# Another order of the set-up, and new planning keys for the first and last steps, in a kernel of memory attention and gated layers on one core

## The chip, the core and the metric

The kernel runs on one core of one Trainium2 chip. A core has TensorE for matrix products, VectorE, ScalarE and GpSimd for elementwise work, and SyncE, which here only issues DMAs; 16 DMA engines move data between the chip's main memory and the on-chip buffers. Matrix products are written to PSUM, eight banks of 128 x 512 f32, and must be copied from there by VectorE or ScalarE. The metric is the device time of one execution in microseconds (us), and smaller is better. In the views PE is TensorE's matmul row, PEld its weight loads, DVE is VectorE, ACT is ScalarE, POOL is GpSimd, SP is SyncE; SPq and ACTq are the DMA issues of SyncE and ScalarE.

## The reference

Four layers are applied to x (2048 x 448) in turn, each with a layer normalization in front and a sum with its input behind: A, B, A, B, the same weights both times.

```python
def _A_ref(x, mem0, Wq, Wk, Wv, Wo, seg_len):      # H = 16 heads, Dh = 256, M = 8, seg_len = 32
    mem = mem0
    for s in range(n_seg):                          # 64 segments, one after the other
        h = concatenate([mem, x[:, 32*s : 32*s+32]], axis=1)
        q, k, v = (einsum('btd,dhe->bhte', h, W) for W in (Wq, Wk, Wv))
        scores = where(mask, einsum('bhqe,bhke->bhqk', q, k) * Dh**-0.5, -1e9)
        o = einsum('bhqk,bhke->bhqe', softmax(scores), v)
        o = einsum('bhte,hed->btd', o, Wo)
        mem = o[:, :M]                              # the next segment's memory
        outs.append(o[:, M:])
def _B_ref(x, W_gate, W_up, W_down):                # F = 1792
    return (relu(x @ W_gate) * (x @ W_up)) @ W_down
```

The memory makes A a recurrence: segment s + 1 can't be scored before segment s has given its eight memory rows.

## The kernel before

**Set-up (`setup`, L672).** Since q and k, and v and Wo, meet only in products, the kernel first multiplies the weights out: M = Wq Wk^T for each head (448 x 448, kept in `Mw` and, for the last 64 of 448 rows, `M3`) and N = Wv Wo for each head (`Nw`). Each of the four weights comes in four quarters of four heads. A quarter of Wq, Wk or Wv is loaded by one transposing DMA (`load_t`, L691, issue L692), a quarter of Wo by a plain one (`load_o`, L695, issue L696). All are issued by SyncE: first Wq and Wk alternately, then Wv and Wo alternately. They land in space that is used for something else later: in `Nw` (Wq, half of Wk, one quarter of Wo) and in `big` (the rest), which later holds the gate layers' weights and the buffer U. TensorE works through M's four quarters (`full` and `pair3`, called from L764 on), then N's (`n_main`, `n_last`, L788 and L796). A unit is one 128 x 448 result in a PSUM bank and one copy by ScalarE (L867) or VectorE (L868). All these matmul groups write a common key, `("stage",)`, so they keep the order of the program among themselves.

**Steps.** Step t works on segment t of the first A layer and, from t = 4 (`LAG`), on segment t - 4 of the second: 68 steps, of which the first four and the last four have one A layer only. A step is: `t_block` (M and M3 times the segment's 40 rows, results TTm and TTs), `s_mem` (scores and softmax of the memory rows, Em and Pm), `p_t_mem` (its transpose PTm), `u_mem` (probabilities times rows, UTm), `un_mem` (112 matmuls of UTm with all of N, L1162), the new memory `mv` (L1180), and `m_t`, which hands it to the next step. Beside that chain the segment's own rows go through `s_seg`, a transposing DMA `PTs` and `u_seg` into U. Every second step does `un` (U times N, 64 rows), a normalization (`ln_b`, whose transposition by DMA is `xBT`) and a gate layer (`b_layer`, `b_down`). In steps 0 and 1 and in the last, `fill` (L969) puts in matmuls of `Mw` with `ident` whose result nobody reads.

**Who sets the order.** All operations are added to `_Order` (L307) in program order, with resources read and written, and `run` places them by a greedy plan with fixed costs per operation: on each engine the operation with the earliest due time goes first among those that can start soon. The due time is `o.key`. A matmul group of a step takes it from the table `SLOT` (L174); the table has keys of their own for steps 0 to 3 (suffix a0 to a3) and for the last four (z0 to z3, z5), and for all others one set of four (0 to 3) that repeats every four steps. Anything without an entry, the DMAs of the set-up among them, is due as early as the earliest of its followers wants, less a latency and its own cost (L374):

```python
o.key = min([q.key - (0.0 if o.kind == q.kind == "pe" else lat + 60.0) for q in o.succs], default=1e9) - min(o.cost.values())
```

From step 8 to 63 the matmul groups are tied to one line in the order of their keys. A change of the matmuls' tile shape (`mode`) is planned at 95 ns.

**Gate weights.** They come in 21 pieces (`S.pieces`, issue L816). A piece is released by a matmul group: in step 0 by those named in `PACE[0]` (L873: p_t_mem, u_mem, un_mem, m_t), in step 1 by most groups. Each also waits until N's groups have read the space (`free`, L785).

Of the kernel before, what the change touches and what calls it, by code (L numbers as in the profile page):

```python
# [6 lines left out]
BF = dt.bfloat16  # L7
# [5 lines left out]
D = 448  # L13
# [16 lines left out]
LAG = 4  # L30
NP = (NSEG + LAG) // 2
# [14 lines left out]
class _Sched:  # L46
# [260 lines left out]
class _Order:  # L307
# [13 lines left out]
    def add(self, kind, eng, cost, fn, rd, wr, name=None, mode=0, lat=None, alt=None, base=(0, 0)):  # L321
# [5 lines left out]
        if kind == "pe" and o.cat:  # L327
            name = o.cat + o.sub
            i = self.count[name] = self.count.get(name, -1) + 1
            o.slot = f"{name}.{i}@" + (f"a{o.t}" if o.t < LAG else f"z{o.t - NSEG}" if o.t >= NSEG else str(o.t % 4))  # L330
# [1118 lines left out]
```

## Time and profile before

| | |
|---|---|
| time, three runs | 1523.01 us median (1522.46 to 1526.68) |
| profiled execution | span 1524.4 us; the page gives no other time of it |
| PE / PEld busy | 1473.0 us (97%) / 1155.9 us (76%) |
| DVE / ACT / POOL busy | 790.8 / 783.1 / 112.3 us |
| mean granted clock of TensorE | 0.993 |
| memory read and written | 10.33 and 1.84 MB |
| first M unit, first unit of N, first t_block of step 1 | at 11.0, 45.0 and 78.98 us |
| steps 8 to 15 | 172.7 us, 21.6 a step |

The profile is of one execution. A row of a timeline reads: start, length, engine, line, operation, out<-in by the program's names, shape, count, and in brackets the idle time before it and what ended it. Most rows bear the line of a helper (L139 for all matmuls, L867 and L868 for copies), so they are told apart by their tiles: `b<-hT,Mw` is a t_block, `b<-Nw,UTm` is un_mem, `b<-big` of 128x448 in the first 72 us is a product of the set-up. A row of a window reads: stretch, length, busy time and count of PE, PEld, DVE, ACT and POOL, TensorE's granted clock, share of the DMA engines, GB/s. An SPq row is the time that SyncE spent issuing a DMA, not the time until it landed. "issue" as releaser means that the profile shows nothing that was waited for.

### The profile page before, as it was taken

The numbers are of one execution on the slowest core, as the hardware profiler recorded it, in microseconds if no ns is written. First come the engines' busy times: TensorE is split into PE (matmuls) and PEld (weight loads), VectorE is DVE, ScalarE is ACT, GpSimd is POOL, SyncE is SP. The second block draws the span as 40 slices with busy tenths as digits, with TensorE's granted clock in tenths as the row PEclk, the third lists the DMA queues.
The fourth block names the chain that finished last, engine by engine and source line by source line (L and its number), as shares of the span: only waits on it lengthen the run. The fifth ranks groups of instructions, "written<-read, shape, count | busy, mean of one in ns | idle before, by whom it ended". The sixth has DMA issues, their size and how long they took to land.

```text
span 1524.4 us, 82710 instructions
## 1 busy us (share of the span) xinstructions
PE 1473.0 (97%) x38178; PEld 1155.9 (76%) x38178; DVE 790.8 (52%) x2131; ACT 783.1 (51%) x2510; POOL 112.3 (7%) x259
## 2 busy tenths in 40 slices
PE   6989899999999999999999999999999999999998
PEld 2567777888787787878787787878777787878786
DVE  5435445645554555545554554545455564555554
ACT  5734554555545555554555455554555555455443
POOL 4000000000000000000000000000000000000000
PEclk9999999999999999999999999999999999999999
DMA  9851011100000101111010110011010110001010
GB/s 212 198 128 25 16 16 21 22 16 18 21 20 15 27 17 21 18 18 22 16 23 17 22 22 16 18 22 22 17 23 17 21 22 14 20 16 20 17 24 15
DMA packets 137738, 47.86 MB, mean 31 GB/s; under 512 B 125736, under 2 KB 137264, under 8 KB 137392
## 3 DMA queue, kind: packets, MB, share of 16 engines
q1 hardware_dynamic: 137040, 42.33, 13.8%
q8 instruction: 300, 4.92, 1.4%
q14 instruction: 46, 0.38, 0.1%
q10 hardware_dynamic: 352, 0.24, 0.1%
HBM read 10.33 MB, written 1.84 MB: 8 GB/s over the span
## 4 chain that ended last, share of the span: by engine, by line
PE 79%; DVE 8%; DMA 7%; SPq 3%; ACT 2%; issue 1%
PE b L139 79%; DMA PTs<-Ps 3%; SPq L692 2%; DMA xBT<-xn 2%; ACT Em L1073 1%; DVE UTm L868 1%; DMA ride<-mv 1%; SPq L1215 1%; ACT Es L1116 1%; DVE stat L1117 1%; DVE big L868 1%; DVE Es L1115 1%; DVE Ps L1119 1%; DMA big<-in_A_Wk_dram 1%; DVE stat L1114 1%
## 5 line engine op out<-in xcount | busy, mean ns | idle before, releaser
L139 PE MATMUL b<-hT,Mw 128*128 128x80 bf16 (+1 forms) x11424 | 438.0, 200 | 0.2 <-issue 0.2
L139 PEld LDWEIGHTS b<-hT,Mw 128*128 128x128 bf16 x11424 | 420.1, 100 | 17.5 <-issue 1.8
L139 PE MATMUL b<-Nw,big 128*32 128x448 bf16 (+1 forms) x3924 | 300.0, 354 | 0.6 <-DMA Nw<-in_A_Wo_dram 0.6
L867 ACT ACTIVATE TTs<-b 128x320 bf16<-128x320 f32 (+5 forms) x670 | 283.3, 423 | 5.3 <-PE b L139 5.0
L867 ACT ACTIVATE TTm<-b 128x80 bf16<-128x80 f32 (+5 forms) x671 | 156.5, 233 | 238.7 <-PE b L139 232.7
L139 PE MATMUL b<-xBT,big 128*128 128x128 bf16 (+3 forms) x4900 | 212.6, 215 | 2.8 <-DMA xBT<-xn 2.0
L139 PEld LDWEIGHTS b<-Nw,big 128*32 128x32 bf16 (+1 forms) x3924 | 129.7, 97 | 99.5 <-issue 10.9
L139 PE MATMUL b<-Nw,UTm 128*32 128x224 bf16 x7504 | 196.8, 263 | 4.2 <-ACT UTm L867 1.6
L139 PEld LDWEIGHTS b<-xBT,big 128*128 128x128 bf16 (+1 forms) x4900 | 184.5, 101 | 19.9 <-issue 3.9
L139 PEld LDWEIGHTS b<-Nw,UTm 128*32 128x32 bf16 x7504 | 178.3, 98 | 25.8 <-DVE UTm L868 13.4
L867 ACT ACTIVATE big<-b 128x512 bf16<-128x512 f32 (+1 forms) x218 | 111.4, 564 | 81.3 <-PE b L139 81.0
L868 DVE CAST TTm<-b 64x64 bf16<-64x64 f32 (+4 forms) x213 | 46.5, 219 | 198.2 <-PE b L139 195.4
L139 PE MATMUL b<-hT,M 64*128 64x80 bf16 (+3 forms) x3808 | 142.1, 197 | 2.9 <-issue 1.2
L868 DVE CAST big<-b 128x512 bf16<-128x512 f32 (+1 forms) x170 | 96.3, 589 | 74.3 <-PE b L139 74.2
L139 PEld LDWEIGHTS b<-hT,M 64*128 64x128 bf16 (+1 forms) x3808 | 105.8, 97 | 28.4 <-issue 11.7
L868 POOL COPY hK<-xn 32x448 bf16<-32x448 bf16 x136 | 75.0, 552 | 580.3 <-DVE xn L921 574.0
L1346 ACT ACTIVATE gT<-b 128x512 bf16<-128x512 f32 (+2 forms) x128 | 66.7, 542 | 82.7 <-PE b L139 48.4
L867 ACT ACTIVATE UTm<-b 128x512 bf16<-128x512 f32 (+2 forms) x158 | 82.7, 554 | 44.5 <-PE b L139 42.1
L139 PE MATMUL b<-big,hB 128*128 128x448 bf16 (+1 forms) x574 | 99.8, 353 | 0.6 <-DVE hB L1347 0.6
L1347 DVE TENSOR_TENSOR hB<-gT,b 128x512 bf16<-128x512 bf16 (+2 forms) x128 | 79.2, 618 | 34.6 <-PE b L139 18.8
L868 DVE CAST TTs<-b 64x256 bf16<-64x256 f32 (+4 forms) x214 | 87.0, 407 | 2.4 <-PE b L139 2.2
L139 PE MATMUL b<-PTs,hK 40*64 40x512 bf16 (+1 forms) x1024 | 77.0, 361 | 10.2 <-DMA PTs<-Ps 7.1
(101 smaller groups left out, 1275.1 us busy)
## 6 DMA issues: line engine op xcount, KB each, us to landing
hK<-mv SPq DMA_DIRECT2D x252, 3.5 KB
big<-in_A_Wo_dram SPq DMA_DIRECT2D x3, 896.0 KB, 5.8
ride<-mv SPq DMA_DIRECT2D x124, 7.0 KB, 1.7
out_dram<-ys SPq DMA_DIRECT2D x32, 56.0 KB, 2.0
big<-in_B_W_up_dram SPq DMA_DIRECT2D x7, 224.0 KB, 2.9
big<-in_B_W_gate_dram SPq DMA_DIRECT2D x7, 224.0 KB, 4.8
big<-in_B_W_down_dram SPq DMA_DIRECT2D x7, 224.0 KB, 4.5
XA<-in_A_x_dram SPq DMA_DIRECT2D x28, 56.0 KB, 2.4
```

What stands on the lines that cost most here:

```text
L139: ins = E.matmul(out, lhsT=lhsT, rhs=rhs, **kw)
L692: S.q.add("dma", ("sp",), {"sp": 6200.0 if w == "Wv" and q else 4100.0}, lambda E: E.dma_start_transpose(out=st[w, q], in_=src[w][:, q * 1 ...
L867: return E.activation(out(), src(), ACT.Copy, **({} if scale is None else {"scale": scale}))
L868: return E.tensor_copy(out(), src()) if scale is None else E.tensor_scalar(out(), src(), scale, None, op0=ALU.mult)
L1073: S.act(lambda E, i=i: E.activation(S.Em[:, i, :], src()[:, i, :], ACT.Exp, bias=st[:, 32 + i:33 + i], scale=1.0, accum_out=st[:, 34 + i:3 ...
L1114: S.dve(lambda E: E.tensor_reduce(st[:, 40:40 + n], src(), AX.X, ALU.max), w, G.res(), [("ss", 0)])
L1115: S.dve(lambda E: E.tensor_tensor(Es, src(), bc(40), ALU.subtract), w, G.res() + [("ss", 0)], [("Es",)])
L1116: S.act(lambda E: E.activation(Es, Es, ACT.Exp), w, [], [("Es",)], 38.0)
L1117: S.dve(lambda E: E.tensor_reduce(st[:, 48:48 + n], Es, AX.X, ALU.add), w, [("Es",)], [("ss", 1)])
L1119: S.dve(lambda E: E.tensor_tensor(dst, Es, bc(56), ALU.mult), w, [("Es",), ("ss", 2)], [("Ps",)])
L1346: S.act(lambda E, g=g, R=R, n=n: E.activation(S.gT[:, g, 0:n], R[0].b()[:, 0:n], ACT.Relu), n, R[0].res(), [("gT", g)])
L1347: S.dve(lambda E, g=g, R=R, n=n, fcs=fcs: E.tensor_tensor(S.hB[:, fcs[0]:fcs[-1] + 1, 0:w], S.gT[:, g, 0:n].rearrange("p (a b) -> p a b", ...
```

## The change

1. The first quarters of Wq and Wk are no longer loaded by transposing DMAs. They come as they lie in memory, in plain DMAs: 384 of the 448 rows in two halves for each weight from SyncE (`load_n`), the last 64 rows of both from ScalarE (`load_l`), into the buffers TTs and UTm, which the steps need only later. TensorE turns them in 128 x 128 blocks by products with the identity (`put`, `put_l`: eight groups of six and one of eight), and ScalarE or VectorE copies them to the places where they lay before. Ahead of that come 24 matmuls of `ident` with itself. The clears of UTm and TTs by GpSimd now wait for those blocks.
2. Wv's and Wo's first quarters are issued ahead of the third and fourth quarters of Wq and Wk, and N's first quarter is computed between M's second and third.
3. The third and fourth quarters of Wq and the last ones of Wv and Wo come in two halves, with keys for each, so that products can start on the first half. The staging places change accordingly.
4. `un_mem` of step 0 is four groups, each waiting for one quarter of N only; the common wait for all of N is gone, and so is the `fill` of step 0. u_seg of step 0 waits for the staging places that its part of U overlaps.
5. Gate pieces in step 0 are released by the last un_mem group and m_t only.
6. The matmul groups of the set-up get entries in `SLOT` (124 of them), steps 4 to 7 get entries of their own (a4 to a7), and the entries of a0 to a3 and z0 to z5 have new values. The entries 0 to 3 of the repeating steps and `BIAS` stay. The planned cost of a mode change is 105 instead of 95 ns.

The diff without the table, cut:

```diff
+SWITCH = 105.0
+WARM = 24
...
-            o.slot = f"{name}.{i}@" + (f"a{o.t}" if o.t < LAG else f"z{o.t - NSEG}" if o.t >= NSEG else str(o.t % 4))
+            o.slot = f"{name}.{i}@" + (f"a{o.t}" if o.t < 2 * LAG else f"z{o.t - NSEG}" if o.t >= NSEG else str(o.t % 4))
...
-        place["Wo", 1] = NW[:, 6 * W8:7 * W8]
+        place["Wo", 1] = BG[:, 6 * W8:7 * W8]
+        hq = {(2, 0): S.N[:, 34:38, :], (2, 1): S.N[:, 42:46, :], (3, 0): S.N[:, 50:54, :], (3, 1): BG[:, 7 * W8:7 * W8 + 4 * D].rearrange("p (k d) -> p k d", k=4)}
...
-        for q in range(4):
-            load_t("Wq", q)
+        def load_n(w, hf):
+            a = slice(512 * hf, 512 * hf + 512)
+            S.q.add("dma", ("sp",), {"sp": 1300.0}, lambda E: E.dma_start(nat[w][:, 0:3072].rearrange("p (k c) -> p k c", k=3)[:, :, a],
+                                                                        dsrc[w][0:384, a].rearrange("(k p) c -> p k c", p=128)),
+                    (), [("nat", w, hf)], name=f"nat{w}{hf}", lat=2500.0)
...
+        for hf in range(2):
+            for w in ("Wq", "Wk"):
+                load_n(w, hf)
+        S.load_x(0, small)
+        for w in ("Wq", "Wk"):
+            load_l(w)
+        load_t("Wq", 1)
+        load_t("Wk", 1)
+        load_t("Wv", 0)
+        load_o(0)
+        for q in (2, 3):
+            for hf in range(2):
+                S.q.add("dma", ("sp",), {"sp": 2050.0}, lambda E, q=q, hf=hf: E.dma_start_transpose(out=hq[q, hf], in_=S.Wq_d[:, 1024 * q + 512 * hf:1024 * q + 512 * hf + 512]),
+                        (), [("Wq", q, hf)], name=f"Wq{q}{hf}", lat=2900.0)
             load_t("Wk", q)
...
+        S.mm(lambda T=T: [MM(T.b()[:, 0:128], S.ident[:, :], S.ident[:, :], start=True, stop=True) for _ in range(WARM)], WARM * 107.0, [("ident",)], T.res() + [("stage",)])
+
+        def put(w, hf):
+            for k in (4 * hf, 4 * hf + 2):
+                T = S.tile("R", 1)
+                S.mm(lambda T=T, k=k: [MM(T.b().bitcast(BF)[:, 384 * j + 128 * kt:384 * j + 128 * kt + 128], nat[w][:, 1024 * kt + 128 * (k + j):1024 * kt + 128 * (k + j) + 128],
+                                          S.ident[:, :], is_transpose=True) for j in range(2) for kt in range(3)], 6 * 80.0, [("nat", w, hf), ("ident",)], T.res() + [("stage",)])
+                S.cp(lambda k=k: st[w, 0][:, k:k + 2, 0:384], lambda T=T: T.b().bitcast(BF)[:, 0:768].rearrange("p (k d) -> p k d", k=2), 768, T.res(),
+                     [(w, 0, k // 2)], speed=3)
...
+        put("Wq", 0)
+        put("Wk", 0)
+        put_l()
+        put("Wq", 1)
+        put("Wk", 1)
+        clear_late()
...
+        m_main(0)
+        m_main(1)
         n_main(0)
-        n_main(1)
-        n_last(1)
         n_last(0)
-        for q in (2, 3):
+        m_main(2)
+        m_main(3)
...
+        for q in (1, 2):
+            load_t("Wv", q)
+            load_o(q, [("Wo", 0)] if q == 1 else [("Wk", q)])
...
+        for q in (1, 2, 3):
             n_main(q)
             n_last(q)
...
-    PACE = {0: ("p_t_mem", "u_mem", "un_mem", "m_t"), 1: ("m_nat", "t_block", "s_mem", "p_t_mem", "u_mem", "un_mem", "m_t", "s_seg", "u_seg", "un")}
+    PACE = {0: ("un_memq3", "m_t"), 1: ("m_nat", "t_block", "s_mem", "p_t_mem", "u_mem", "un_mem", "m_t", "s_seg", "u_seg", "un")}
...
-        if t < 2 or t == NSTEP - 1:
+        if t == 1 or t == NSTEP - 1:
...
+            for q in range(4):
+                S.q.sub = f"q{q}"
+                S.mm(lambda q=q: part(q), 7 * S.pitch(DH) + 5.0, [("UTm", w, 0), ("UTm", w, 1)] + [("UW", c) for c in range(4)] + [("N", kt * 16 + u) for kt in range(3) for u in (2 * q, 2 * q + 1, 2 * q + 8, 2 * q + 9)] +
+                     [("N", 48 + 2 * q), ("N", 49 + 2 * q)], C.res() + [("mem",)], mode=2)
```

`m_main(q)` is the old loop over M's units for one quarter, with its `pair3` groups behind both head pairs instead of behind each; `part(q)` is 28 of un_mem's 112 matmuls, those of the heads whose N comes from quarter q.

More of the change, by code (lines that the diff above doesn't have):

```diff
@@ L442, in run @@
                     continue
-                sw = {o: 95.0 if e == "pe" and mode not in (o.mode, o.alt) else 0.0 for _, o in lst}
+                sw = {o: SWITCH if e == "pe" and mode not in (o.mode, o.alt) else 0.0 for _, o in lst}
                 lim = min(x + sw[o] for x, o in lst) + (BIAS.get("win", 60.0) if e == "pe" else 40.0)
@@ L730, in setup @@
                   [("ident",), ("sel", 8)], [("sel", j)])
-        S.pool(lambda E: E.memset(S.UTm[:, :, :], 0.0), 3600, (), [("UTm", w, l) for w in range(2) for l in range(2)] + [("UW", c) for c in range(4)])
+        pass
         S.pool(lambda E: E.memset(S.Pm[:, :], 0.0), 128, (), [("Pm",)])
@@ L778, in setup @@
         S.Nkeys = [("N", o) for o in range(NO)]
-        for q in range(4):
-            load_t("Wv", q)
-            load_o(q, [("Wk", q)] if q > 1 else [])
         sizes = {"Wu": 6, "W3": 2, "Wg": 6, "Wd": 7}
@@ L876, in mm @@
         q = self.q
-        due = bool(self.pieces) and q.cat in self.PACE.get(q.t, ())
+        due = bool(self.pieces) and (q.cat if q.t else q.cat + q.sub) in self.PACE.get(q.t, ())
         if due and q.cat == "t_block":
@@ L1249, in u_seg @@
                  [("PTs",)] + [("hKx", pp, s, l) for l in range(l0, l1)] + [("hKm", pp, s, l, n) for l in range(l0, l1) for n in range(2)],
[L1250 removed]
+                 [r for l in R for r in R[l].res()] + [key[l][1] for l in R] + (S.stage[c] + [("Uz",)] if t == 0 else []), mode=3)
             for l in range(l0, l1):
```

118 lines of the change are left out of this document (80 added, 38 removed), and 274 rows, old and new, of the table SLOT.

## The prediction

> **What bounds the kernel now.** I read the page first, then SyncE's DMA issues and TensorE's rows of the first 80 us, then the same steps as windows.
>
> ```profile
> span 1524.4 us, 82710 instructions
> ...
> PE 1473.0 (97%) x38178; PEld 1155.9 (76%) x38178; DVE 790.8 (52%) x2131; ACT 783.1 (51%) x2510; POOL 112.3 (7%) x259
> ...
> DMA  9851011100000101111010110011010110001010
> ```
>
> TensorE is busy 97% of the span, so time can go only where it idles, runs at half clock or works for nothing. The 16 DMA engines are full in the first two slices (38 us each) only: the set-up. SyncE's issues there:
>
> ```profile
> 16.41 3.92 SPq L692 DMA_TRANSPOSE Nw<-in_A_Wq_dram  x1
> 20.38 4.44 SPq L692 DMA_TRANSPOSE big<-in_A_Wk_dram  x1
> 24.86 5.11 SPq L692 DMA_TRANSPOSE Nw<-in_A_Wq_dram  x1
> 30.01 3.95 SPq L692 DMA_TRANSPOSE big<-in_A_Wk_dram  x1
> ...
> 38.79 0.59 SPq L696 DMA_DIRECT2D big<-in_A_Wo_dram  x1
> 39.43 6.67 SPq L692 DMA_TRANSPOSE big<-in_A_Wv_dram  x1
> ```
>
> A quarter of Wq, Wk or Wv is 448x1024 bf16, 0.917 MB, and holds the queue for about 4.05 us. A quarter of Wo is issued in 0.59 us but makes the next transpose 2.6 us longer (6.67 against 4.05): 3.2 us.
>
> TensorE in the same time, two rows of its timeline, then two windows (length, busy time of PE, PEld, DVE, ACT, POOL, clock, DMA share, GB/s):
>
> ```profile
> 28.99 2.01 PE L139 MATMUL b<-big,Nw 128*128 128x448 bf16 x6 [4.08 <-DMA big<-in_A_Wk_dram]
> ...
> 78.98 0.40 PE L139 MATMUL b<-hT,M 64*128 64x40 bf16 x18 [0.33 <-DVE hT L868]
> ```
> ```profile
> 43.30:71.50 28.20, 27.61 (x352) 15.98 (x352) 13.45 (x31) 20.71 (x50) 0.00 (x0) 1.00 0.86 201
> 71.50:79.00 7.50, 5.80 (x167) 4.23 (x167) 2.60 (x10) 2.41 (x8) 0.02 (x1) 1.00 0.40 89
> ```
>
> M's product begins at 11.0 us, stands 4.08 us for the fifth key transpose and ends at 43.3. From there TensorE is full: N's four quarters, with step 0's t_blocks (5.6 us of hT,Mw and hT,M rows) between them, until 71.5. Only then run step 0's softmax, u_mem and un_mem, whose 7.5 us hold no other useful work (the six Mw,ident matmuls there only keep TensorE busy, and go), and step 1 starts at 78.98. So the set-up is bound by the key DMAs up to 30 us, by TensorE up to 71.5, by one chain up to 79.
>
> The last place is steps 1 to 7. Windows from one memory update to the next, steps 4 to 7, then four steady steps:
>
> ```profile
> 152.20:171.40 19.20, 16.48 (x466) 13.60 (x462) 10.53 (x30) 10.34 (x35) 2.74 (x6) 0.91 0.09 18
> 171.40:195.60 24.20, 22.37 (x677) 17.71 (x677) 11.41 (x30) 10.93 (x35) 0.19 (x1) 1.00 0.06 13
> 195.60:215.00 19.40, 17.36 (x472) 13.96 (x468) 9.61 (x27) 10.80 (x38) 2.40 (x5) 0.91 0.21 26
> 215.00:239.00 24.00, 23.37 (x529) 16.60 (x526) 7.80 (x23) 10.93 (x36) 0.47 (x2) 1.00 0.05 9
> 239.00:325.40 86.40, 85.66 (x2232) 68.34 (x2230) 45.60 (x121) 45.73 (x148) 5.89 (x14) 1.00 0.09 20
> ```
>
> Steps 4 to 7 leave 7.2 us idle, steady ones 0.74. Steps 1 to 3 leave 1.7, 2.3 and 1.0. Windows at 80.7, 101.2, 166.0 and 210.4 show clock 0.50 for 3.3 us; each such stretch of full work loses half of that, 1.7 us.
>
> **The change, part by part.** *Key DMAs.* Two transposes (8.1 us) become six plain loads of the same bytes, 1.83 MB, four from SyncE and two from ScalarE's queue. The gate weights' plain loads, rows of 1.8 KB, go out six in 3.97 us, 1.38 MB: 340 GB/s; Wo's rate is 287. That gives 5.4 to 6.4 us; I take 5.7, all in by about 8.5. The order on SyncE follows the due times: by hand the four wide loads come first (-93, -76, -40, -40), then Wq1 and Wk1 (-37), Wv0 and Wo0, Wk2, the Wq2 halves, Wk3, the Wq3 halves. Wv0 and Wo0 thus pass the last key quarters and cost them 4.05 + 3.2 us. Issue of the last key half ends at 0.7 + 5.7 + 7 x 4.05 + 3.2 = 38.0; transposes land 2.5 us after issue (Wk3: 33.96 to 36.4), so it is there by 40.5, Wk3 and the half ahead of it by 38.5.
>
> *TensorE transposes.* There are 8 x 6 + 8 = 56. The four of xn took 0.61 us together at the start's low clock: 0.15 each there, half of that at full clock. So 4.3 to 8.5 us; I take 5, beside the loads. Their copies are 10 of 512 to 768 columns; by the xAT copy (0.60 us for 512 on ScalarE) and the PTs copy (0.42 on VectorE) some 7 us over two engines, beside the transposes. The 24 warming matmuls lie in the 6 us in which TensorE waits anyway. M's first quarter starts near 10 and is done before M's second can start (Wk1 lands near 17). Nothing here sets the end.
>
> *M and N.* A quarter of M is 5.8 us (16.17 to 19.06 us is half of one), of N 5.5. M's second quarter runs 17 to 23, N's first waits for Wo0 (near 24.5) and ends at 30, M's third follows at 30.5 to 36.5, its fourth is bound by the halves: it ends at 44, against 43.3 now, with a quarter of N done.
>
> *From M's end to step 1.* Now: 28.2 + 7.5 = 35.7 us. After: three quarters of N 16.5, the same t_blocks 5.6, and beside N what was in the tail: s_mem, s_seg, p_t_mem and u_mem 1.65 and three quarters of un_mem (2.87 x 3/4 = 2.15). Then the rest: N's last copy 0.6, the last un_mem quarter 0.72, and 1.47 from un_mem's end to step 1 (77.51 to 78.98). Sum 28.7, step 1 at 72.7: **-6.3 us**. DMA does not bind it: Wv1, Wo1, Wv2, Wo2, Wv3, Wo3 need 4 + 3 x 3.2 + 2 x 4.05 more queue time, to 60, and the last 5 us to land, 65; then 2.8 us of N are left, at 67.8, and TensorE needs until 69.9. N's second quarter waits for Wo1 until 47.7; t_blocks cover that, without them it costs 3.7. The step-0 pieces of the gate weights fall from four to two; their first reader is at 120.9 us, the last now lands by 101, so that costs nothing.
>
> *Clears.* UTm's and TTs's clears (3.1 + 0.95 + 1.0 us on GpSimd) wait for the transposes, from 9 us instead of 3. Behind them on GpSimd stand hK and hS copies that u_mem and s_seg read after 50 us: nothing.
>
> *Order of steps 1 to 7.* No row shows the new order. Upper bound: all idle above the steady step's 0.2, 11.4 us, and four stretches, 6.8. Lower bound: as much again lost. The nearest row is steps 1 to 3, which already had keys of their own and idle 1.66 a step against 1.96 in steps 4 to 7 with shared keys: 4 x 0.3 = 1.2, and one stretch avoided, 1.7. I take **-3**. *End steps:* step 64 idles 2.2 us and has a half-clock stretch, the last 14 us idle 5.2 in one serial chain (un, normalization, gate layer). They had own keys already: between -4 and +2, I take **-0.7**. *SWITCH* moves only which of ScalarE and VectorE copies in steady steps; TensorE's order there is a fixed line and its idle 0.74 in 86.4: 0, between -2 and +2.
>
> Sum -10.0. The profiled execution spans 1524.4, 1.4 above the median 1523.01 of the runs; carried over as a difference: **1513**.
>
> **A rule against the change.** The tile view of ident gives the xn transposes a median of 311 ns each, but four start within 0.3 us: they overlap. The Trainium skill, "TensorE: Matmul & The Clock Gate", section "Part 4: PE-mode transpose", gives about 275 ns for one in a kernel and says that transposes do not raise the clock; by it 56 would be an estimated 15.4 us. What that would do here is the second rival.
> The stretch at 166 us followed waits of at most 0.94 us, in sum 3 us within 9. The same page, section "Why this matters for your kernels", puts the drop at idle gaps over about 3 us; the trace here disagrees. By the rule the new set-up's waits of 1 to 2 us cost no clock; by the row each may cost 1.7, which the next wait for a DMA swallows.
>
> **Rivals.** (a) *Order gains little and the passed key quarters bind.* If Wk3 and Wq3 land 3 us later (Wo0 in their way at its 287 GB/s, plain loads no faster than transposes), set-up gives -3.3, the rest -0.5: 1519. For it: the DMA engines are full already. Against: step 0's chain goes beside N in any case. 15%.
> (b) *Transposes run one by one.* 56 x 0.311 = 17.4 us from 6.5 on, then M at half clock for 3.4 us: M's end moves to about 54, as M and N0 follow without a gap (23.9 + 1.7 + 23.2 + 5.5). Step 1 starts at 83: +4; with -3.7 elsewhere, 1523. 4%.
> (c) *Slower: the new order of steps 1 to 7 makes TensorE wait in the memory chain.* Softmax, transpose and copy waits (Pm, PTm, UTm, mv) are what it idles on now, 1.1 us each in a step; if every step waits twice as long and three more stretches fall to half clock, +12.8 + 5 against -7: 1534. It decides once steps 1 to 7 idle more than 24 us in place of 12.8. For it: the orders are scattered due times of a planner with fixed costs. Against: its costs served the steady steps. 7%.
> (d) *The new order of steps 4 to 7 comes near the steady steps:* -10 there with the stretches gone, -7 in the set-up and end: 1506. 19%.
> (e) *It doesn't do what it says:* the Wk loads are due close behind Wq1 and Wk1 (-40 against -37); issued after these, M starts at 17 and loses 2 to 3 us: 1516. Counted in the forecast.
>
> **How the numbers follow.** Forecast with (e) 55%: 1509 to 1517.5. The range reaches over (d) and (a), 1503 to 1520. A measurement of this kernel can tell about 0.3%, 4.6 us, from no change: faster below 1518.4 takes the forecast, (d) and a third of (a), 79%; same the rest of (a), (b) and a little between, 14%; slower 7%.
>
> **What would show it.** Right: step 1's first t_block near 72.7 us; M's end near 44 with N rows before M's second half; no 4 us wait at 25 to 29; un_mem in four pieces; steps 4 to 7 idle about 5 us. Wrong: M starting after 17, a wait of over 3 us for Wo1 or Wq3, or more idle in steps 1 to 7 than the 12.8 us of now.

## The result, and the profile after

The changed kernel takes 1516.64 us (median of 7 runs, 1514.59 to 1519.04) beside 1523.14 us for the kernel before (7 runs, 1520.42 to 1528.76): 0.9951 times as long, 95% interval 0.9935 to 0.9966, or 6.5 us less. Beside the last experiments it was measured once more: 1516.09 against 1524.98 us, 0.9938 (0.9922 to 0.9954). The forecast was 1513, in a range of 1503 to 1520.

The page of the changed kernel, with the row of its instruction queue:

```profile
span 1514.8 us, 82643 instructions
...
PE 1469.2 (97%) x38132; PEld 1157.9 (76%) x38132; DVE 789.0 (52%) x2120; ACT 787.3 (52%) x2531; POOL 112.8 (7%) x259
...
DMA  9951101001110101001010100011010100101010
...
q8 instruction: 300, 4.92, 1.3%
```

The span is 9.6 us shorter, 3 us more than the medians differ, so the differences of these two profiles overstate the gain. Cut at the memory updates (`mv`) of steps 0, 8 and 63, in us:

| | to step 0's update | step 0 to 8 | 8 to 63 | 63 to the end |
|---|---|---|---|---|
| before | 77.9 | 161.0 | 1190.6 | 94.8 |
| changed | 83.1 | 149.3 | 1190.5 | 92.0 |
| difference | +5.2 | -11.7 | -0.1 | -2.8 |

So the set-up lost time in this execution, and the steps under the new keys won more. The steady steps stayed. Between the updates of steps 0 and 8 both kernels do nearly the same work; one window each of TensorE alone, before and then changed (length, busy time with the number of matmuls, granted clock, DMA share, GB/s):

```profile
77.90:239.00 161.10, 147.61 (x4242) 0.96 0.20 44
83.10:232.40 149.30, 141.00 (x4238) 0.99 0.23 51
```

Of the 11.8 us, 5.2 are idle time and 6.6 are busy time of almost the same matmuls. Four half-clock stretches of 3.4 us lie in the first window (from 80.7, 101.1, 166.0 and 210.4 us), one in the second (from 166.1), so a part of the gain is clock.

SyncE's issues in the set-up of the changed kernel (start, length):

```profile
2.84 10.23 SPq L767 DMA_TRANSPOSE Nw<-in_A_Wq_dram  x1
13.12 3.81 SPq L767 DMA_TRANSPOSE Nw<-in_A_Wk_dram  x1
16.97 5.39 SPq L767 DMA_TRANSPOSE big<-in_A_Wv_dram  x1
...
33.98 4.75 SPq L767 DMA_TRANSPOSE big<-in_A_Wk_dram  x1
38.77 2.91 SPq L802 DMA_TRANSPOSE Nw<-in_A_Wq_dram  x1
41.72 1.55 SPq L802 DMA_TRANSPOSE big<-in_A_Wq_dram  x1
```

The first transposing DMA holds the queue for 10.23 us, where before none of the first five took more than 4.00. It stands behind the four wide loads, the last of which landed at 9.27; the two loads of the last rows, from ScalarE, landed at 13.33 and 14.24. The last key half is issued at 43.27 and lands at 46.2; before, the last key quarter had landed at 36.1.

TensorE's timeline of the changed kernel, the rows with the long waits and the landmarks:

```profile
4.91 1.22 PE L141 MATMUL b<-ident,TTs 128*128 128x128 bf16 x12
14.46 0.26 PE L141 MATMUL b<-ident,ys 8*128 8x8 bf16 x4 [8.33 <-DMA ys<-in_A_mem_dram]
14.65 1.46 PE L141 MATMUL b<-ident,UTm 128*128 128x128 bf16 x12
...
16.43 2.34 PE L141 MATMUL b<-ident,TTs 128*128 128x128 bf16 x20
18.57 1.22 PE L141 MATMUL b<-ident,UTm 128*128 128x128 bf16 x12
19.62 11.16 PE L141 MATMUL b<-Nw 128*128 128x448 bf16 x88
...
43.66 2.46 PE L141 MATMUL b<-big,Nw 128*128 128x448 bf16 x18 [1.80 <-DMA Nw<-in_A_Wq_dram]
...
50.88 0.55 PE L141 MATMUL b<-hT,M 64*128 64x40 bf16 x30 [1.34 <-DVE M L1013]
...
58.91 0.19 PE L141 MATMUL b<-hT,Mw 128*128 128x40 bf16 x1 [3.69 <-issue]
...
59.37 6.46 PE L141 MATMUL b<-big 128*128 128x448 bf16 x22
...
79.79 2.87 PE L141 MATMUL b<-Nw,UTm 128*32 128x224 bf16 x112
...
84.23 0.42 PE L141 MATMUL b<-hT,M 64*128 64x40 bf16 x20 [0.43 <-DVE hT L1013]
```

M begins at 19.62 instead of the forecast 10, and ends at 49.5 (the row before 50.88) instead of 44. In the middle of step 0's t_blocks TensorE stops for 3.69 us, and the profile names nothing that it waited for. All 112 matmuls of un_mem run in one go behind N, not beside it. Step 1 starts at 84.23; the forecast was 72.7.

Windows of the changed kernel: from M's end to step 1, then the four that the prediction calls steps 4 to 7 (they run from the update of step 4 to that of step 8, so they hold steps 5 to 8), then four steady steps (length, then busy time of PE, PEld, DVE, ACT and POOL, granted clock, DMA share, GB/s):

```profile
49.50:84.20 34.70, 29.26 (x487) 17.83 (x485) 14.21 (x48) 20.85 (x57) 2.63 (x2) 0.90 0.64 143
152.97:171.34 18.37, 15.75 (x445) 13.11 (x437) 10.20 (x31) 9.82 (x33) 2.75 (x6) 0.91 0.18 19
171.34:190.09 18.75, 18.29 (x525) 14.31 (x529) 7.88 (x21) 10.48 (x35) 0.19 (x1) 1.00 0.06 12
190.09:209.13 19.04, 18.99 (x625) 15.83 (x613) 13.16 (x36) 11.44 (x40) 0.37 (x2) 1.00 0.14 23
209.13:232.38 23.25, 22.82 (x523) 16.33 (x524) 8.38 (x23) 10.45 (x35) 2.50 (x6) 1.00 0.07 15
232.40:318.80 86.40, 85.86 (x2233) 68.38 (x2231) 45.45 (x122) 45.53 (x147) 5.88 (x14) 1.00 0.09 20
```

The four windows from step 4's update to step 8's take 79.41 us with 3.6 idle; the same four of before took 86.8 with 7.2. The window of four steady steps is alike in both. The second of those four is the largest difference: 24.20 us before, 18.75 now. Part of that is work that moved (the 140 matmuls `b<-xBT,big` of a gate layer now run one window later), but the later window did not grow: 19.40 before, 19.04 now. It took them in where it had 2.0 us of idle time and a half-clock stretch.

### The profile page after: what moved, and what is told of

The parts are those of the page before. It is cut to its first block, busy times and chain, and to the rows that moved or that the text cites. A ratio compares the mean times of both kernels' runs of the same rounds, so it can differ in the third digit from the quotient of the medians.

```text
span 1514.8 us, 82643 instructions
## 1 busy us (share of the span) xinstructions
PE 1469.2 (97%) x38132; PEld 1157.9 (76%) x38132; DVE 789.0 (52%) x2120; ACT 787.3 (52%) x2531; POOL 112.8 (7%) x259
## 3 DMA queue, kind: packets, MB, share of 16 engines
q1 hardware_dynamic: 131520, 42.07, 14.3%
## 4 chain that ended last, share of the span: by engine, by line
PE 77%; DVE 8%; DMA 7%; SPq 4%; ACT 3%; issue 1%
PE b L141 77%; DMA PTs<-Ps 4%; DMA xBT<-xn 2%; SPq L767 2%; DVE UTm L1013 1%; ACT Em L1218 1%; DVE big L1013 1%; SPq L1376 1%; DMA ride<-mv 1%; DVE stat L1262 1%; DVE Ps L1264 1%; ACT Es L1261 1%; DVE Es L1260 1%; DVE stat L1259 1%; DVE stat L1216 0%
## 5 line engine op out<-in xcount | busy, mean ns | idle before, releaser
L141 PE MATMUL b<-Nw,big 128*32 128x448 bf16 (+1 forms) x3772 | 294.5, 353 | 0.3 <-ACT big L1012 0.3
L141 PEld LDWEIGHTS b<-Nw,big 128*32 128x32 bf16 (+1 forms) x3772 | 125.9, 96 | 95.7 <-issue 10.9
L141 PE MATMUL b<-Nw,UTm 128*32 128x224 bf16 x7504 | 193.4, 260 | 1.7 <-DVE UTm L1013 0.7
L141 PE MATMUL b<-hT,M 64*128 64x80 bf16 (+2 forms) x3808 | 141.9, 197 | 2.5 <-DVE M L1013 1.3
L1012 ACT ACTIVATE UTm<-b 128x448 bf16<-128x448 f32 (+2 forms) x157 | 82.2, 554 | 47.6 <-PE b L141 45.5
L1508 DVE TENSOR_TENSOR hB<-gT,b 128x512 bf16<-128x512 bf16 (+2 forms) x128 | 79.1, 619 | 29.9 <-PE b L141 15.9
```

The costliest lines, as they stand in the source:

```text
L141: ins = E.matmul(out, lhsT=lhsT, rhs=rhs, **kw)
L1012: return E.activation(out(), src(), ACT.Copy, **({} if scale is None else {"scale": scale}))
L1508: S.dve(lambda E, g=g, R=R, n=n, fcs=fcs: E.tensor_tensor(S.hB[:, fcs[0]:fcs[-1] + 1, 0:w], S.gT[:, g, 0:n].rearrange("p (a b) -> p a b", ...
```

## The experiments

Each was timed against the kernel before on the same chip. The table gives the ratio of the times and, from one profiled execution each, the stretches of the table above. The stretch from step 8 to 63, which no edit was meant to touch, varies between 1189 and 1195 us over these executions; a difference of a few us between two profiles is therefore no effect by itself. Nor is the profiled execution always a typical one: it lies 3.6 to 4.7 us above the median of its kernel's runs in memory_load_first, old_setup_all_new_keys, old_setup_new_steps_4_to_7 and rows_from_sync_un_beside_n, and 3.9 us below it in change_with_95. In the edits shown, entries of `SLOT` stand by themselves; in the kernels there are several to a line. Lines of code are cut behind the part that changes.

| kernel | ratio (95%) | to step 0's update | 0 to 8 | 8 to 63 | 63 to the end |
|---|---|---|---|---|---|
| old_setup_new_steps | 0.9974 (0.9961 to 0.9987) | 80.0 | 152.7 | 1191.3 | 97.4 |
| new_setup_old_steps | 1.0035 (1.0019 to 1.0052) | 81.4 | 159.6 | 1189.0 | 97.1 |
| un_beside_n | 0.9957 (0.9940 to 0.9974) | 83.8 | 149.7 | 1191.4 | 92.6 |
| memory_load_first | 0.9966 (0.9949 to 0.9984) | 87.1 | 151.4 | 1192.6 | 92.0 |
| old_setup_all_new_keys | 0.9977 (0.9961 to 0.9993) | 78.7 | 153.9 | 1192.6 | 101.8 |
| memory_and_rows_from_sync | 0.9944 (0.9926 to 0.9962) | 78.7 | 153.4 | 1193.7 | 92.4 |
| warming_72 | 0.9971 (0.9957 to 0.9984) | 85.1 | 153.0 | 1190.0 | 93.3 |
| old_setup_new_steps_4_to_7 | 0.9956 (0.9941 to 0.9971) | 78.2 | 155.2 | 1194.1 | 96.1 |
| old_setup_all_keys_and_105 | 0.9952 (0.9938 to 0.9966) | 80.1 | 152.0 | 1189.9 | 94.4 |
| change_with_95 | 0.9996 (0.9981 to 1.0011) | 81.2 | 149.9 | 1190.4 | 97.0 |
| rows_from_sync_un_beside_n | 0.9936 (0.9920 to 0.9953) | 80.5 | 150.7 | 1195.2 | 91.4 |
| change_again | 0.9938 (0.9922 to 0.9954) | 78.9 | 151.5 | 1190.3 | 91.8 |

### Whose gain is it: set-up or keys?

**old_setup_new_steps:** the kernel before, with the changed kernel's entries a1 to a7.

```diff
-    "t_block0f.0@a1": 60377,
+    "t_block0f.0@a1": 125518,
...
-            o.slot = f"{name}.{i}@" + (f"a{o.t}" if o.t < LAG else
+            o.slot = f"{name}.{i}@" + (f"a{o.t}" if o.t < 2 * LAG else
```

> The kernel before with the new planning keys of steps 1 to 7 alone (own keys for steps 4 to 7 too); set-up, step 0 and end steps as before. Theory: the whole gain of the change comes from the keys, of the early steps above all. Between the memory updates of step 0 and of step 8 before took 161.0 us and after 149.3; if the keys did that, it is about 149 to 151 here, step 0's update stays near 78 us, and the time is 10 to 12 us below before (near 1512). Rival: the early steps became shorter because of the new set-up (gate weights in another order, work left over from step 0); then the stretch stays near 161 and the time within 3 us of before.

Steps 0 to 8 went from 161.0 to 152.7 us without any of the new set-up, and the time fell by 0.26%. So the larger part of the 11.7 us that the changed kernel shows there belongs to the keys alone. The theory had more: 149 to 151 us, and a time 10 to 12 us below before, where it is some 4. In this profile step 0's update and the end both came later than before.

**new_setup_old_steps:** the counterpart, the changed kernel with the old entries a1 to a3, none for steps 4 to 7, and the old z entries. One entry of step 2 (un_mem) stays new, and both halves of Wo's last quarter wait for Wk's, to keep the order of the DMAs. The planned cost of a mode change stays at 105 ns.

```diff
-            o.slot = f"{name}.{i}@" + (f"a{o.t}" if o.t < 2 * LAG else
+            o.slot = f"{name}.{i}@" + (f"a{o.t}" if o.t < LAG else
```

> The changed kernel with the old keys of steps 1 to 7 (shared ones for 4 to 7) and of the end steps; one key of step 2's un_mem keeps its new value, so that the set-up's DMAs go out in the changed kernel's order. Theory: the new set-up alone loses; step 0's memory update is near 83 us against 77.9, the rest takes as long as before, and the time is 4 to 6 us above before (near 1528). Rival (the forecast's): the new set-up gains 6 us; then 1517.

Slower than before by 0.35%: without the new keys of the steps the new set-up gains nothing. (What 105 ns do with the old keys was not run apart, so a part of the loss can be theirs.) Step 0's update comes at 81.4 us, 3.5 later than before, steps 0 to 8 take nearly what they took, and the stop of TensorE inside the t_blocks is there again (3.53 us from 53.75).

**old_setup_new_steps_4_to_7:** the same as the first, but a1 to a3 stay old too.

```diff
+    "t_block0f.0@a4": 42963, "t_block0r.0@a4": 49811, "t_block0r.1@a4": 45807,
...
+    "b_down.6@a7": 17241,
```

> The kernel before with the changed kernel's keys for steps 4 to 7 only. Theory (most of what steps 1 to 8 gain is the seventh step, 24.2 us with the shared keys and 18.75 with its own, as old_setup_new_steps had it too): steps 0 to 8 take 154 to 156 us, 5 to 6 less than before, ratio 0.9965 to 0.998. Rival (the keys of steps 1 to 3 gain it, and the later steps only take over their lead): 158 to 161 us, ratio 0.999 to 1.0005.

155.2 us, as the theory had it, and a ratio a little below what it gave: by the runs these keys alone gain what the whole change gains, within the intervals (0.9956 against 0.9951 and 0.9938). The second of the four windows, from the update of step 5 to that of step 6, in its trace:

```profile
172.13:190.88 18.75, 18.30 (x525) 14.30 (x529) 7.89 (x22) 10.49 (x35) 0.19 (x1) 1.00 0.11 13
```

It is the changed kernel's window to the hundredth (18.75 us, 525 matmuls) in a kernel whose set-up and steps 1 to 3 are the old ones. By the runs, the new entries of steps 1 to 3 add nothing that can be told (0.9974 with them, 0.9956 without; the intervals overlap).

### What holds the set-up up?

**memory_load_first:** the key of the group that reads `mem` is made early, and by it its two loads go ahead of the loads of x in ScalarE's queue, so that the wait of 8.33 us for `ys` goes.

```diff
-    "prep.0@a0": 168510,
+    "prep.0@a0": -80000,
```

> The changed kernel with the two small loads of the initial memory first on ScalarE's queue, ahead of the key rows, so that their transpose doesn't hold TensorE until 14.5 us. Theory: that wait of 8.3 us is off the path, since the third and fourth key quarters land when they do (the last at 46.2 us): M's first quarter begins near 10 to 12 instead of 19.6, M still ends at 49 to 50, and step 0's memory update stays within 1 us of 83.1. Rival: the wait sets what follows; then M's end and step 0's memory update come 4 to 8 us earlier.

The wait stayed and took another name. TensorE's row in this kernel:

```profile
19.39 2.31 PE L141 MATMUL b<-ident,TTs 128*128 128x128 bf16 x20 [8.60 <-DMA TTs<-in_A_Wk_dram]
...
22.77 11.40 PE L141 MATMUL b<-Nw 128*128 128x448 bf16 x88
```

It now waits 8.60 us for the last 64 rows of Wk, which ScalarE issues behind the loads of x and which landed at 19.3. The load of `mem` was not what set M's start; it was one of several small loads that share the DMA engines with the first transposing DMA. Neither the theory nor the rival had what followed. M began at 22.77 and ended at 57.3 us, and step 0's update came at 87.1, 4 us later than in the changed kernel. The transposing DMAs were slower in this execution (10.99 us for the first, 6.51 for the second), and the last key half landed at 52.0. Why they were slower stays open.

**memory_and_rows_from_sync:** both sets of small loads early, the rows of Wq and Wk from SyncE.

```diff
-    "prep.0@a0": 168510, "prepc.5@a0": 147510,
+    "prep.0@a0": -80000, "prepc.5@a0": -70000,
...
-            S.q.add("dma", ("act",), {"act": 600.0}, lambda E: E.dma_start(nat["Wq"][r, 3072:4096]
+            S.q.add("dma", ("sp",), {"sp": 600.0}, lambda E: E.dma_start(nat["Wq"][r, 3072:4096]
```

> The changed kernel with the memory loads first in ScalarE's queue and the two loads of the last 64 rows of Wq and Wk issued by SyncE ahead of Wk's wide loads. Theory (the first transposing DMA is slow, 10.2 us, because plain loads of a second queue are still running beside it): Wq's second quarter is issued in 6 us or less and lands 2 to 4 us earlier than in the changed kernel, M ends at 46 to 47 us in place of 49.5, and the time is 2 to 3 us below the changed kernel's (ratio 0.993 to 0.994). Rival (the same bytes have to be moved, whatever the queue): the first transposing DMA ends within 1 us of where it does in the changed kernel, M ends at 49 to 51 us, and the ratio is 0.995 to 0.997.

The first transpose is issued in 7.28 us instead of 10.23. But it starts 1.6 us later (4.44 to 11.72), behind the two loads that moved to SyncE, so that it ends 1.35 us earlier and lands at 14.3 instead of 15.9. M begins at 14.77, 5 us earlier than in the changed kernel, and yet ends at the same time:

```profile
14.77 11.62 PE L141 MATMUL b<-Nw 128*128 128x448 bf16 x88
26.95 5.59 PE L141 MATMUL b<-big 128*128 128x448 bf16 x32 [0.56 <-DMA big<-in_A_Wo_dram]
33.16 3.03 PE L141 MATMUL b<-big,Nw 128*128 128x448 bf16 x21 [0.63 <-DMA Nw<-in_A_Wq_dram]
...
42.61 4.13 PE L141 MATMUL b<-big,Nw 128*128 128x448 bf16 x18 [3.82 <-DMA Nw<-in_A_Wq_dram]
46.57 2.45 PE L141 MATMUL b<-big 128*128 128x448 bf16 x18
```

The five microseconds come back as waits for Wo and for the halves of Wq, the last of 3.82 us, and the 18 matmuls behind it ran at half clock (4.13 us for what took 2.46 in the changed kernel). The transpose came out between the theory (6 us or less, landing 2 to 4 us earlier) and the rival (ending within 1 us): the loads of the second queue may have a part in its length, but that is not shown apart from the wide loads of its own queue, which landed at 9.27 in the changed kernel and at 10.74 here. On what it is worth the theory was wrong: M ended at 49.9, in the rival's 49 to 51. The ratio, 0.9944, does not differ from the changed kernel's.

**change_again** shows the other side, one window of PE alone from M's start to its end (length, busy time, clock, DMA share, GB/s):

```profile
21.30:49.40 28.10, 28.10 (x211) 1.00 1.13 224
```

> The changed kernel itself, beside the others on one chip. Expected: ratio 0.994 to 0.996 as measured at first; the stop before matmul 473 at 55 us and the half-clock stretch behind it come again (3 to 4 us), if they belong to the program and not to that one execution.

Here M started at 21.40, every key was there in time, and TensorE was busy for 28.10 us of 28.10. The ratio, 0.9938, lies just below what I had expected, and the stop at 55 us came again with 1.17 us instead of 3.7; the half-clock stretch lay ahead of it this time (from 52.55 us). So M's end near 49.5 has two bounds of the same size: M's start plus 28.1 us of products (M and N's first quarter), and the landing of the last key half at 44 to 46 us. Mending one shows the other.

**un_beside_n:** u_mem of step 0 and the four un_mem groups get keys ahead of N's last groups; 84 of un_mem's 112 matmuls then run between N's.

```diff
-    "u_mem.0@a0": 195568,
+    "u_mem.0@a0": 60000, "un_memq0.0@a0": 60400, "un_memq1.0@a0": 60500, "un_memq2.0@a0": 60600, "un_memq3.0@a0": 60700,
```

> The changed kernel with earlier keys for step 0's u_mem and four un_mem groups, so that three of the four run between N's last groups; the DMAs' order is the same. Theory: the forecast's step that moved un_mem beside N failed only because u_mem came last by its key; now 28 instead of 112 un_mem matmuls stand behind N, step 0's memory update comes 1.5 to 2.5 us earlier than the changed kernel's 83.1, and the time falls by as much, to 8 to 9 us below before. Rival: switches of the matmul shape and the copies between N's groups eat it: within 0.7 us of 83.1.

Step 0's update did not come earlier (83.8 us, with a stop of 3.63 us beside the changed kernel's 3.69), and the ratio does not differ from the changed kernel's: the rival. **rows_from_sync_un_beside_n** joins both mends:

```diff
-    "prep.0@a0": 168510, "u_mem.0@a0": 195568,
+    "prep.0@a0": -80000, "u_mem.0@a0": 60000,
...
```

> memory_and_rows_from_sync with the keys of un_beside_n: both mends of the set-up together. Theory (the set-up is bound by the key transfers up to M's end and by the chain of step 0 behind N): step 0's memory update comes at 76 to 77 us in place of 78.7, and the ratio is 0.992 to 0.9935. Rival (between M's end and step 1 TensorE always has work, so that moving un_mem beside N only swaps it with the t_blocks): 78 to 79 us, ratio as memory_and_rows_from_sync, 0.9935 to 0.995.

80.5 us and 0.9936, beside 78.9 and 0.9938 for the changed kernel on the same chip. The update came later than either had it, 1.3 us of it with a longer stop (1.79 us, against 0.49 in memory_and_rows_from_sync); nothing is gained, as the rival had it. From M's end on TensorE has work in any order, and taking un_mem forward only puts something else behind it.

### The stop at 55 us

In the changed kernel's DMA rows from 55 to 59 us (forty slices of 0.1 us) one packet is not data:

```profile
GB/s 294 289 294 289 287 287 287 289 289 297 287 292 294 448 274 138 108 33 27 18 27 9 36 74 115 28 17 19 28 8 36 45 358 376 224 81 358 394 367 385
...
q1 hardware_dynamic: 2140, 0.76, 105.5%
q8 instruction: 1, 0.02, 1.6%
```

The queues carry only 8 to 138 GB/s from 56.5 to 58.2 us, and 290 at the start of the row. The packet of the instruction queue, 16,384 bytes, started at 56.37 and took 1.01 us; TensorE went on at 58.91. The page counts 300 such packets; for its 2 x 38,132 matmuls and weight loads that is one for about 254 instructions, or 127 matmuls with their loads. **warming_72** asks whether the stop belongs to the place in the program or to the work:

```diff
-        S.mm(lambda T=T: [MM(T.b()[:, 0:128], S.ident[:, :], S.ident[:, :], start=True, stop=True) for _ in range(WARM)], WARM * 107.0,
+        S.mm(lambda T=T: [MM(T.b()[:, 0:128], S.ident[:, :], S.ident[:, :], start=True, stop=True) for _ in range(72)], WARM * 107.0,
```

> The changed kernel with 72 in place of 24 matmuls of ident with itself at the start, in the same order otherwise; the 48 more lie in TensorE's wait for the memory load. Theory (the stop of 3.7 us at 55.2 us, for which the profile shows nothing, is TensorE waiting for its own instructions): the stop moves by about 96 instructions, to some 129 matmuls of the burst of t_block matmuls in place of 177, or disappears, since it is tied to the place in the program and not to the work. Rival (it is a hidden wait for data or for the clock): it stays behind the same matmul, 177 of the burst, with 3 to 4 us. In both the time is within 0.3% of the changed kernel.

Its t_blocks:

```profile
52.41 0.54 PE L141 MATMUL b<-hT,M 64*128 64x40 bf16 x30 [1.34 <-DVE M L1013]
52.89 1.62 PE L141 MATMUL b<-hT,Mw 128*128 128x40 bf16 x57
54.45 0.42 PE L141 MATMUL b<-hT,M 64*128 64x40 bf16 x20
54.80 0.73 PE L141 MATMUL b<-hT,Mw 128*128 128x40 bf16 x22
59.59 0.59 PE L141 MATMUL b<-hT,Mw 128*128 128x40 bf16 x13 [4.07 <-issue]
```

30 + 57 + 20 + 22 = 129 matmuls of the burst, then the stop; in the changed kernel it came behind 177. The 48 matmuls put in at the start moved it by 48 of the work and left it at the same place of the program: counted from TensorE's first matmul it lies behind the 473rd in both. In all nine profiles with the new set-up there is a stop at that place, of 0.49 to 4.07 us, with "issue" as releaser where I read its row. Four of them:

| | packet starts, takes | stop ends | behind the packet's end |
|---|---|---|---|
| changed kernel | 56.37, 1.01 | 58.91 | 1.53 |
| warming_72 | 57.10, 1.11 | 59.59 | 1.38 |
| memory_and_rows_from_sync | 54.12, 1.14 | 56.72 | 1.46 |
| change_again | 54.41, 1.16 | 56.98 | 1.41 |

change_again has three more stops without a releaser in its first 130 us, behind the 1106th, 1361st and 1994th matmul (0.61, 0.87 and 1.26 us). They lie 633, 255 and 633 matmuls apart, 5, 2 and 5 times about 127, and each ends 1.3 to 1.4 us after such a packet. So the stops keep the spacing of the packets: TensorE waits for its own instructions, and at the 473rd matmul goes on 1.4 to 1.5 us after the packet is through. How long it stands depends on when that packet starts, between 54.12 and 57.10 us in the table. Why it starts 2 us earlier in some executions stays open.

### The end of the kernel

**old_setup_all_new_keys:** old_setup_new_steps with the new z entries besides.

```diff
-    "t_block0f.0@z3": 130669, "t_block0r.0@z3": 108428,
+    "t_block0f.0@z3": -7278, "t_block0r.0@z3": -715,
...
```

> The set-up of before with the changed kernel's keys for steps 1 to 7 and for the last steps. Theory (the two tables of keys gain, each on its own, and the new set-up loses): steps 0 to 8 take 152 to 153 us as in old_setup_new_steps, and from step 63 to the end 92 us in place of 97.4, so 7 to 9 us below before, ratio 0.994 to 0.9955, which is below the changed kernel. Rival (the end's gain belongs to the state in which the changed kernel arrives there, not to its keys): the end stays at 95 to 97 us and the ratio at 0.997.

The ratio stayed at 0.9977, the rival's, but the end grew to 101.8 us in the profiled execution, which neither had. What the edit lacked was the planned cost of a mode change, which I had put down at nothing. In the plan with 95 ns ScalarE's copies and normalization sums come in another order in the last steps, and SyncE issues an output transfer ahead of the last transposition `xBT<-xn`. **old_setup_all_keys_and_105** adds it:

```diff
-                sw = {o: 95.0 if e == "pe" and mode not in (o.mode, o.alt) else 0.0 for _, o in lst}
+                sw = {o: 105.0 if e == "pe" and mode not in (o.mode, o.alt) else 0.0 for _, o in lst}
...
-                    c += 95.0
+                    c += 105.0
```

> old_setup_all_new_keys with the planned cost of a mode change raised from 95 to 105 ns as in the changed kernel. Theory (the new end keys were found together with the 105; with 95 the plan puts the transposition of the last xBT behind an output transfer, and the end took 101.8 us): from step 63 to the end 92 to 94 us, the half-clock stretch at 1501 us is gone, steps 0 to 8 take 153 us again, and the time is 7 to 9 us below before, ratio 0.994 to 0.9955. Rival (the end depends on how the steps before it arrive, and the changed kernel's arrival is what it needs): 96 us or more, ratio 0.997 to 0.999.

94.4 us and 0.9952, the half-clock stretch at 1501 gone: the theory, but for 0.4 us. The intervals of the two ratios still overlap a little (0.9961 to 0.9966). **change_with_95** is the change without it:

```diff
-SWITCH = 105.0
+SWITCH = 95.0
```

> The changed kernel with the planned cost of a mode change put back to 95 ns. Theory (the 105 is needed by the end keys): from step 63 to the end 97 to 102 us in place of 92.0, the rest as in the changed kernel, ratio 0.998 to 1.001. Rival (a planned cost 10 ns apart only swaps copies of engines that have time): 92 to 93 us at the end, ratio within 0.001 of the changed kernel's.

0.9996 and 97.0 us at the end: without the 10 ns the change gains nothing that can be measured, beside 0.9938 with them on the same chip. The medians are 8.1 us apart; the two profiles show 6.1 of it, 5.2 at the end. The last window, from step 66's update to the end, with 105 (change_again):

```profile
1480.70:1512.40 31.70, 27.59 (x781) 18.58 (x779) 15.67 (x36) 11.48 (x39) 0.18 (x1) 1.00 0.06 14
```

With 95 (change_with_95), and in it the row behind which the clock fell:

```profile
1481.60:1518.50 36.90, 29.63 (x781) 18.84 (x779) 15.48 (x36) 11.57 (x39) 0.18 (x1) 0.95 0.05 12
```
```profile
1494.21 0.40 PE L141 MATMUL b<-ident,Ps 128*128 128x128 bf16 x4 [1.73 <-DVE Ps L1264]
```

TensorE waits there for the probabilities `Ps`, which VectorE makes. Two of VectorE's rows with 95, then two with 105 (change_again):

```profile
1493.30 0.63 DVE L1059 BATCH_NORM_STATS2 stat<-XB 128x6 f32<-128x448 bf16 x1
1493.85 0.31 DVE L1264 TENSOR_TENSOR Ps<-Es,stat 128x160 bf16<-128x160 f32 x1
```
```profile
1490.49 0.18 DVE L1263 RECIPROCAL stat<-stat 128x4 f32<-128x4 f32 x1
1490.70 0.33 DVE L1264 TENSOR_TENSOR Ps<-Es,stat 128x160 bf16<-128x160 f32 x1
```

With 105 `Ps` follows its reciprocal at once; with 95 two additions and the statistics of a normalization stand between, and TensorE waits 1.73 us. The same holds with the old set-up: 1.73 us of wait for `Ps` in old_setup_all_new_keys, none in old_setup_all_keys_and_105. So the plan's order on VectorE is the first step of what the 10 ns decide.

The two windows, with 781 matmuls in each, are 5.2 us apart: 2.0 of it in slower matmuls (29.63 against 27.59; a half-clock stretch from 1495.6), 3.2 in more idle time.

## Why the prediction was right, and where it was not

The time was right within 4 us (-10.0 us was forecast, -6.5 and -8.9 were measured), but the sum was put together from terms that were wrong in both directions. That they cancel is luck.

- **Key DMAs: the step that failed.** I had the last key half issued at 38.0 us and M's end at 44. They came at 43.27 and 49.5. Of the 5.3 us, 2.6 are the wide loads and the first transpose (13.07 against 0.7 + 5.7 + 4.05 = 10.45), 1.3 Wv's quarter (5.39 against 4.05), 0.7 Wk's last, the rest smaller. Wo's term held: 0.58 and 6.68 us against 3.2 + 4.05. I had priced loads and transposes one after the other, each by its rate alone, and all six loads in by 8.5. The wide ones were in at 9.27, beside the loads of x, which I had left out; the last rows, from ScalarE, landed at 13.33 and 14.24, beside the first transpose, which was issued until 13.07. No run separates the shares of these neighbours in the 2.6 us. (Wk's last quarter, from which I took 2.5 us to land, landed at 36.05 and not at 36.4, which makes it 2.1; the last half took 2.9.)
- **TensorE transposes: the size was near, the place wrong.** The 56 took about 6 us (rows of 1.22, 1.46, 2.34 and 1.22; forecast 5, between 4.3 and 8.5). The first twelve ran at 4.91, but the other 44 stood in TensorE's order behind the products of `ys` and ran from 14.65 on, so that M began at 19.62 (21.40 in change_again) and not at 10. "Nothing here sets the end" was wrong: from there on TensorE needs 28.1 us, to 49.5. I had followed the four wide loads and had not asked when the small loads of ScalarE's queue land, behind four loads of x.
- **From M's end to step 1: right in size, by another way.** Forecast 28.7. From M's last product it was 34.7 in the first profile and 30.6 in change_again (49.41 to 80.04). The stop took 3.7 and 1.2 us of it. The half-clock stretch near it cost 2.2 us in the first, nearly all in the 22 products of N behind the stop (6.46 us; 4.32 in change_again), and 0.7 in the second, where it fell on t_block matmuls of 40 columns (4.8 us for the 172 that took 4.1 in the first). That leaves 34.7 - 3.7 - 2.2 = 28.8, and 30.6 - 1.2 - 0.7 = 28.7. (The forecast counts the 35.7 of before from the first t_block, 1.0 us behind M's last product; counted so, 27.4 is left in both.) But un_mem did not run beside N, since u_mem's own key (195568) put it behind everything, and un_beside_n shows that moving it is worth nothing. The prediction said that un_mem would come in pieces beside N; I had taken the order from the waits that the change removes, and not from the keys, which decide it.
- **The stop.** No term of mine had it. Before, it stood in the trace as 1.17 us with "issue" at 98.26, beside an instruction packet at 97.18.
- **Set-up, all in all:** forecast -6.3. The change shows +5.2 and +1.0 in its two profiles, and with the old keys of the steps, and 105 ns, the kernel was 5.4 us slower than before by the runs. Whether it gains anything with the new keys is open: old_setup_all_keys_and_105 and change_again, on one chip, differ by 2.2 us in their medians, and their intervals overlap.
- **Steps 1 to 7: the right sign, a third of the size.** Forecast -3, measured -11.7 and -9.5 up to step 8's update (-10.9 and -8.7 up to step 7's), and -7 to -9 in the three kernels that have these keys with the old set-up. I had counted on one half-clock stretch less; in the change there are three less. Rival (d) had this mechanism: steps 4 to 7 near the steady ones. I had sized the term by steps 1 to 3 as the nearest row. That row said what older keys of their own were worth, not what new ones could be; the steady window, which I took as the far bound, was nearer. Most of it comes from the keys of steps 4 to 7 (-5.8 us in old_setup_new_steps_4_to_7). A slip in the reading: the windows shown as steps 4 to 7, with 7.2 us idle, are those of steps 5 to 8; the 12.8 us for steps 1 to 7 are counted rightly.
- **End and mode cost.** Forecast -0.7 and 0. The end gave -2.8 and -3.0 against the profile of before, and 4 to 6 against the three other profiles with old z entries, which took 96.1 to 97.4. The mode cost, "it moves only which engine copies in steady steps", decides the order in the last steps and is worth 5.2 us of the profile there, the larger part of 8.1 us between the medians. In the steady stretch of these two profiles it is nothing (1190.4 and 1190.3 us), as forecast.
- **The rule of the Trainium skill.** The rule in "TensorE: Matmul & The Clock Gate", "Part 4: PE-mode transpose" (about 275 ns each, no rise of the clock) was rival (b). The trace decides against the rival: a transpose lasted up to 0.31 us, but twelve of them took 1.46 us, 0.12 each, at half clock (14.65 us), since they overlap. The clock rose at 19.36, after 4.9 us in which TensorE had done nothing but transposes and 0.26 before the first product of M; in warming_72 it rose 0.71 before it. M's late start had another cause.

So (a) came true for the keys, larger than I had put it, and (d) for the steps. The forecast lay between them, and the time did too: the set-up came out 7 to 12 us worse than forecast, the steps and the end 9 to 11 better.

## What to carry to other kernels

Follow every operand of the first matmul to its landing, in the small loads of the second queue as well, and ask what each loading queue does to a transposing DMA beside it. When a planner orders the work, read the order from its keys and costs: a key can undo the freedom that a removed wait gives, and 10 ns in a planned cost can decide the last steps. An idle time with no releaser in a dense burst of small matmuls, with a packet of the instruction queue beside it, was TensorE out of instructions here; shifting the program by a few matmuls tests it.

## What the runs showed of the hardware

- TensorE can run out of instructions while the DMA engines are full: stops of 0.49 to 4.07 us at one fixed place of the program, ended, in the four profiles of the table, 1.4 to 1.5 us after a 16,384-byte instruction packet; further stops in change_again lie at whole multiples of about 127 matmuls from it.
- The transposing DMA of a quarter took 10.23 us to issue behind four plain loads of its own queue and beside plain loads of another, 7.28 with two of the latter ahead of it in its own queue, and 3.65 to 4.00 for the first five of the kernel before, where only the loads of x and mem ran beside the first.
- The same half clock cost unlike amounts: 18 matmuls of 448 columns took 4.13 us instead of 2.46, while 172 of 40 columns took 4.8 instead of 4.1 with the clock at half for 3.1 us of it.
- 48 more matmuls that nobody reads cost nothing where they stood (a wait of 7.39 us for a load was still left behind them), but shifted where instructions ran out: the ratio was 0.9971 (0.9957 to 0.9984), above the second measurement of the change (at most 0.9954) and within reach of the first (at most 0.9966); its stop was the longest, 4.07 us.
- A half-clock stretch of 3.4 us came at 166 us in the changed kernel too, behind waits of 0.53, 0.90 and 0.74 us within 2.8 us, much as before; the rule of the Trainium skill on this ("TensorE: Matmul & The Clock Gate", "Why this matters for your kernels": gaps over about 3 us) does not explain it.
